# Group normalization on one core: stores and loads issued in runs of two tiles in place of one by one

## The chip, the cores and the metric

One NeuronCore of a Trainium2 chip runs the whole kernel. The metric is the device time in microseconds (us), the median of several executions. The profile is of a single execution, recorded by the hardware profiler; its span (first to last instruction) is 1.7 us shorter than the device time of that execution. With one core there is no second die to compare with. A run counts as slow when it is more than 1.5% above the fastest of its kernel.

## The reference

```python
# x: (128, 1024, 32, 16) bf16, g and b: (1024,) bf16
def reference(x, g, b):
    G = 32
    xr = x.reshape(B, G, C // G, H, W)
    mu = xr.mean(axis=(2, 3, 4), keepdims=True)
    var = ((xr - mu) ** 2).mean(axis=(2, 3, 4), keepdims=True)
    xn = (xr - mu) / jnp.sqrt(var + 1e-5)
    return xn.reshape(B, C, H, W) * g[None, :, None, None] + b[None, :, None, None]
```

Each of the 4096 groups (128 images, 32 groups) has 16,384 values that lie next to each other. Every value is read once and written once: 134.2 MB in, 134.2 MB out.

## The kernel before

The kernel works on 32 tiles. A tile is 4 images by 32 groups, so 128 partitions of 16,384 bf16 values, 4 MB. There are six tile buffers, and a tile is normalized in place: it is loaded into its buffer, worked on there, and stored from it. A buffer can take the next load only when its store has landed.

- PE sums a tile by multiplying it with an identity matrix; DVE reduces the sum to the mean.
- ACT squares the tile in two halves and accumulates.
- POOL and DVE scale 29 of the 32 channels; ACT scales the last three between the two halves of the next tile's squares.
- SP issues every large load and store, in the order of the program. It is one queue in two senses: SP waits in order, and in every trace of this study the large transfers land in the order in which they were issued. Each of them is spread over the core's 16 DMA engines.

The part that sets this order:

```python
XBUFS = 6
UPFRONT = 6
AHEAD = 5
# ...
    for i in range(min(UPFRONT, NT)):      # NT = 32 tiles
        L(i)                               # load a tile
# ...
    def finish(i):                         # called in the middle of ACT's squares of tile i + 1
        if i < 0 or in_parts(i):           # the last two tiles are stored in quarters, elsewhere
            return
        for k in range(KC - LAST_SHARE, KC):
            scale_on("act", i, k)
        S(i, 0, NQ)                        # store the tile
        state.pop(i)
        j = i + AHEAD
        if UPFRONT <= j < NT:
            L(j)
# ...
    for i in range(NT):
        Q(i)                               # squares of tile i; inside it, finish(i - 1)
        if i + 1 < NT:
            M(i + 1)                       # sums of tile i + 1 on PE
            R0(i + 1)                      # its mean on DVE
        V(i)                               # 1/std, scale and shift of tile i
        A(i)                               # scaling on POOL and DVE
```

With S for store and L for load, SP's order is S0, S1, L6, S2, L7, S3, L8 and so on. L7 goes into the buffer of tile 1 and so waits for S1; L6 and S2 stand in the queue between the two. This number of transfers between a store and the load that waits for it is called the cushion below. It is what the DMA engines still have to do when the load is issued. Here it is two.

## Time and profile before

| | |
|---|---|
| device time | 634.2 us |
| span of the profiled execution | 631.9 us |
| share of the span in which the data queue keeps the 16 DMA engines busy | 99.0% |
| busiest computing engine | ACT, 85% |
| rate in mid-span (100 to 550 us) | 432 GB/s |

First some lines of the profile page of the kernel before: busy time by engine; the busy tenths of the DMA engines and what they moved, in 40 slices of the span; the data queue with its share of 16 engines; and the large DMA issues with their median time from issue to landing.

```profile
PE 293.1 (46%) x1025; PEld 114.4 (18%) x1025; DVE 380.2 (60%) x645; ACT 539.0 (85%) x268; POOL 346.8 (55%) x523
...
DMA  8999999999999999999999999999999999999996
GB/s 365 431 437 423 430 431 429 431 433 431 424 430 432 431 431 429 430 433 438 428 432 429 433 431 429 430 430 433 434 431 431 430 430 432 433 426 436 433 418 271
...
q1 hardware_dynamic: 10944, 268.44, 99.0%
...
xt<-in_x_dram SPq DMA_DIRECT2D x30, 4096.0 KB, 29.3
out_dram<-xt SPq DMA_DIRECT2D x30, 4096.0 KB, 38.3
```

No computing engine is full, the DMA engines are. Slices 2 and 3 hold only loads, the middle alternates, the last three hold only stores (the very last also the end, when engines finish), and the rate shows no pattern in this. The same by stretch, from the table of windows of the kernel before (length, then busy time of each engine, the granted clock of PE, the DMA share, GB/s):

```profile
60.00:100.00 40.00, 16.62 (x57) 6.34 (x56) 27.80 (x46) 39.82 (x17) 25.67 (x39) 0.66 1.00 428
100.00:550.00 450.00, 213.12 (x738) 82.58 (x737) 285.44 (x454) 401.73 (x195) 274.86 (x408) 0.72 1.00 432
```

The Trainium skill ("DMA: Bandwidth & Descriptors", Where 436 GB/s comes from) gives the ports a ceiling of 435.2 GB/s; 432 is 99% of that. The "HBM Reference" (Specifications (TRN2)) says that a core that streams alone gets about 425 GB/s, bounded by its 16 DMA engines; the profile's mean over the whole span, start and end included, is 425.

Next, SP's own waits in mid-span (150 to 540 us; total, times, longest) and a piece of SP's timeline (start, duration, instruction), both of the kernel before:

```profile
SPq L101 <- DMA out_dram<-xt: 366.8, 20, 19.0
SPq L381 <- DVE xt L368: 1.5, 1, 1.5
```

```profile
299.30 0.34 SPq L101 DMA_DIRECT2D xt<-in_x_dram  x1
299.75 0.37 SPq L381 DMA_DIRECT2D out_dram<-xt  x1
318.67 0.34 SPq L101 DMA_DIRECT2D xt<-in_x_dram  x1
319.12 0.37 SPq L381 DMA_DIRECT2D out_dram<-xt  x1
```

SP waits nearly always at a load, for a store to land; a store is ready when its turn comes. The store of 299.75 lands after 38.3 us, near 338.1, and the load that waits for it is issued at 338.11. A long wait of SP is no loss by itself here: when it ends, the DMA engines still have two transfers to work on.

PE shows the rhythm in which tiles arrive. Its timeline before (the bracket is its idle time before the piece and what ended that):

```profile
289.61 9.74 PE L166 MATMUL pa<-xt,eye 128*128 128x512 bf16 x32 [10.28 <-DMA xt<-in_x_dram]
309.01 8.58 PE L166 MATMUL pa<-xt,eye 128*128 128x512 bf16 x32 [9.67 <-DMA xt<-in_x_dram]
328.35 9.15 PE L166 MATMUL pa<-xt,eye 128*128 128x512 bf16 x32 [10.75 <-DMA xt<-in_x_dram]
```

One tile comes every 19.4 us, the time of one load and one store.

### The profile page before, as it was taken

How to read it: one execution, taken by the hardware profiler on the slowest of the kernel's cores; microseconds unless marked ns; L12 is line 12 of the kernel's file. 1: busy time of each engine (PE TensorE's matmuls, PEld its weight loads, DVE VectorE, ACT ScalarE, POOL GpSimd, SP SyncE). 2: the span in 40 equal slices, each digit the busy share in tenths (PEclk: the TensorE clock that was granted, in tenths of full speed). 3: DMA queues.
4: the chain of work that ended last, by engine and by line, in shares of the span. 5: the costliest groups of instructions: out<-in, count | busy, mean ns of one | idle time of the engine just before them, and what ended most of it. 6: DMA issues, size and time to landing. Idle time of an engine off the chain costs nothing.

```text
span 631.9 us, 3907 instructions
## 1 busy us (share of the span) xinstructions
PE 293.1 (46%) x1025; PEld 114.4 (18%) x1025; DVE 380.2 (60%) x645; ACT 539.0 (85%) x268; POOL 346.8 (55%) x523
## 2 busy tenths in 40 slices
PE   5578604553245633456433565335553345647000
PEld 2233201221112211122111222112221112213000
DVE  1087666666676576545775457754657654577660
ACT  4589999999999897877997779977989797797960
POOL 0077666666666576544775446764557654477100
PEclk9689758766787657876678766677865788658655
DMA  8999999999999999999999999999999999999996
GB/s 365 431 437 423 430 431 429 431 433 431 424 430 432 431 431 429 430 433 438 428 432 429 433 431 429 430 430 433 434 431 431 430 430 432 433 426 436 433 418 271
DMA packets 11063, 268.70 MB, mean 425 GB/s; under 512 B 1312, under 2 KB 1312, under 8 KB 1312
## 3 DMA queue, kind: packets, MB, share of 16 engines
q1 hardware_dynamic: 10944, 268.44, 99.0%
q8 instruction: 8, 0.13, 0.1%
q14 instruction: 15, 0.12, 0.0%
q10 hardware_dynamic: 96, 0.00, 0.0%
HBM read 134.22 MB, written 134.22 MB: 425 GB/s over the span
## 4 chain that ended last, share of the span: by engine, by line
DMA 67%; ACT 15%; PE 7%; issue 4%; DVE 3%; POOL 0%; SPq 0%; DVEq 0%; ACTq 0%; POOLq 0%
DMA out_dram<-xt 42%; DMA xt<-in_x_dram 25%; ACT ja L244 13%; PE pa L166 7%; DVE xt L368 3%; ACT xt L363 2%; DMA gb_b<-in_g_dram 1%; POOL scl L337 0%; SPq L101 0%; ACT rstd L308 0%; DVE rstd L312 0%; DVE jd L189 0%; POOL shift L343 0%; DVEq L455 0%; DVE bia L324 0%
## 5 line engine op out<-in xcount | busy, mean ns | idle before, releaser
L244 ACT ACTIVATE ja<-xt,negmean 128x8192 fp8e5<-128x8192 bf16 x60 | 426.7, 7112 | 52.1 <-DVE jd L189 52.0
L166 PE MATMUL pa<-xt,eye 128*128 128x512 bf16 x976 | 281.8, 460 | 289.7 <-DMA xt<-in_x_dram 278.5
L368 DVE TENSOR_SCALAR xt<-xt,scl,bia 128x512 bf16<-128x512 bf16 x536 | 352.6, 732 | 40.0 <-POOL bia L353 40.0
L368 POOL TENSOR_SCALAR xt<-xt,scl,bia 128x512 bf16<-128x512 bf16 x390 | 308.7, 806 | 3.4 <-POOL bia L353 0.3
L166 PEld LDWEIGHTS <-eye 128*128 128x128 bf16 x1024 | 114.3, 114 | 468.5 <-DMA xt<-in_x_dram 290.6
L337 POOL TENSOR_SCALAR scl<-gb,rstd 128x32 f32<-128x32 f32 x31 | 11.2, 361 | 218.2 <-DVE rstd L312 218.2
L189 DVE TENSOR_SCALAR_CACHE_REDUCE jd<-pa 128x512 bf16<-128x512 f32 x32 | 22.0, 688 | 149.0 <-PE pa L166 149.0
L363 ACT ACTIVATE xt<-xt,bia,scl 128x512 bf16<-128x512 bf16 x98 | 72.0, 798 | 0.8 <-DVE bia L324 0.8
L244 ACT ACTIVATE ja<-xt,q 128x4096 fp8e5<-128x4096 bf16 x8 | 29.6, 3706 | 6.6 <-DVE jd L189 6.4
L312 DVE RECIPROCAL rstd<-rstd 128x1 f32<-128x1 f32 x32 | 5.1, 160 | 35.8 <-ACT rstd L308 35.8
L343 POOL TENSOR_SCALAR shift<-scl,negmean 128x32 f32<-128x32 f32 x31 | 11.2, 360 | 3.1
L216 POOL TENSOR_SCALAR off<-negmean,q 128x1 f32<-128x1 f32 x2 | 0.9, 432 | 20.5 <-DVE jd L189 20.5
L166 PE MATMUL pb<-xt,eye 128*128 128x512 bf16 x48 | 11.6, 388 | 1.0 <-DMA xt<-in_x_dram 1.0
L308 ACT ACTIVATE rstd<-s,v 128x1 f32<-128x1 f32 x30 | 8.8, 294 | 2.8
L244 ACT ACTIVATION_READ_ACCUMULATOR ja<-xt,negmean 128x1 f32 x60 | 11.2, 187 | 0.0
L353 POOL TENSOR_TENSOR bia<-shift,gb 128x32 f32<-128x32 f32 x31 | 7.8, 252 | 2.6
L308 ACT ACTIVATE rstd<-var,eps_t 128x1 f32<-128x1 f32 x2 | 0.6, 295 | 9.2 <-DVE jv L292 9.2
L273 POOL TENSOR_SCALAR v<-s 128x1 f32<-128x1 f32 x30 | 5.8, 192 | 2.5
L156 DVE COPY gb<-gb_p 128x64 f32<-128x64 f32 x1 | 0.2, 224 | 5.6 <-PE gb_p L148 5.6
L116 ACT ACT_TABLE_LOAD x1 | 1.3, 1283 | 1.7 <-PEq L444 1.7
L189 DVE DVE_READ_ACCUMULATOR jd<-pa 128x1 f32 x32 | 2.6, 81 | 0.0
L292 DVE TENSOR_SCALAR_CACHE_REDUCE jv<-sq,seed 128x4 f32<-128x4 f32 x2 | 0.4, 216 | 2.7 <-ACT ja L244 2.7
(18 smaller groups left out, 6.1 us busy)
## 6 DMA issues: line engine op xcount, KB each, us to landing
xt<-in_x_dram SPq DMA_DIRECT2D x30, 4096.0 KB, 29.3
out_dram<-xt SPq DMA_DIRECT2D x30, 4096.0 KB, 38.3
xt<-in_x_dram SPq DMA_DIRECT2D x8, 1024.0 KB, 16.5
out_dram<-xt SPq DMA_DIRECT2D x8, 1024.0 KB, 17.8
gb_b<-in_g_dram ACTq DMA_DIRECT2D x1, 2.0 KB, 3.2
gb_b<-in_b_dram ACTq DMA_DIRECT2D x1, 2.0 KB, 5.3
```

Source lines behind the costliest of these rows:

```text
L116: chain("act", nc.scalar.activation(out=warm[:], in_=eps_t[:], func=ACT.Sqrt))
L166: nc.tensor.matmul(out=ps[:], lhsT=eye[:], rhs=st["xt"][:, k * MMN : (k + 1) * MMN], start=(k == lo), stop=(k == hi - 1),),
L189: nc.vector.tensor_scalar(out=jd[:], in0=ps[:], scalar1=-inv_n, scalar2=seed, op0=ALU.mult, op1=ALU.add, accum_out=total[:],),
L244: nc.scalar.activation(out=ja[:, 0:w], in_=st["xt"][:, k * w : (k + 1) * w], func=ACT.Square, bias=bias, scale=scale, accum_out=sq, satura ...
L273: nc.gpsimd.tensor_scalar(out=v0[:], in0=s0[:], scalar1=inv_n, scalar2=EPS, op0=ALU.mult, op1=ALU.add,),
L308: nc.scalar.activation(out=rstd[:], in_=last_sum[:], func=ACT.Sqrt, bias=bias[:], scale=scale),
L312: chain("dve", nc.vector.reciprocal(out=rstd[:], in_=rstd[:]))
L337: nc.gpsimd.tensor_scalar(out=scl[:], in0=gam, scalar1=rstd[:], scalar2=None, op0=ALU.mult),
L343: nc.gpsimd.tensor_scalar(out=shift[:], in0=scl[:], scalar1=st["negmean"][:], scalar2=None, op0=ALU.mult,),
L353: nc.gpsimd.tensor_tensor(out=bia[:], in0=shift[:], in1=bet, op=ALU.add),
L363: inst = nc.scalar.activation(out=span, in_=span, func=ACT.Identity, bias=bia, scale=scl)
L368: inst = eng.tensor_scalar(out=span, in0=span, scalar1=scl, scalar2=bia, op0=ALU.mult, op1=ALU.add,)
```

## The change

The intent is to turn the DMA engines' direction half as often: two stores in a row, then two loads in a row.

```diff
 XBUFS = 6
 UPFRONT = 6
-AHEAD = 5
+RUN = 2
@@
         S(i, 0, NQ)
         state.pop(i)
-        j = i + AHEAD
-        if UPFRONT <= j < NT:
-            L(j)
+        if i % RUN == RUN - 1:
+            first = i + 1 + UPFRONT - RUN
+            for j in range(first, min(first + RUN, NT)):
+                L(j)
```

SP's order becomes S0, S1, L6, L7, S2, S3, L8, L9. L6 waits for S0 and L7 for S1, so only one transfer is left between a store and its load.

## The prediction

> **What bounds the kernel now.** The DMA engines. The page gives their data queue 99.0% of the span of 16 engines; by stage (busy time by window) the DMA share is 1.00 from 100 to 550 us at 431 to 433 GB/s, against 85% for ACT, 60% for DVE. The Trainium skill ("DMA: Bandwidth & Descriptors", Where 436 GB/s comes from) puts the port ceiling at 435.2 GB/s; the trace's 431 agrees. 268.44 MB at 431 GB/s are 623 us of the 632 us span; the rest is start, a thinning end (share 0.95 to 0.17 from 622 to 630 us, engines finishing apart) and the last landing.
>
> **Does a change of direction cost anything now?** In the packet records one engine's share of a tile is 8 packets of 1.213 us; landings follow each other every 9.68 us in the alternating stretch, every 9.70 us in the opening loads, which all go one way: no cost per switch to save. By stage, pure loads (12 to 56 us) show 436 GB/s, alternation 431 to 432, pure stores (584 to 622) 417 to 430: no pattern. Slow packets cluster at some switches (the first, near 58 us, about 0.9 us per engine), but all excess over 1.2135 us averages 2.7 us per engine for the run, part of it beside instruction fetches that stay. Halving the switches gives back about 1 us at most.
>
> **What moves.** No work is added or removed; the order on SP becomes S0 S1 L6 L7 S2 S3 L8 L9. Even tiles' loads keep their place, odd ones go one transfer earlier (9.7 us). A load waits on SP for the store 6 tiles back to land (the skill, same page, Anatomy of one DMA: the wait is on the issuing sequencer, the engines just drain their queues; the queue's waits agree: 425 us, 26 times). Now the second load waits for the store just two transfers ahead of it. At its issue only the first load is still queued: 9.7 us of work, where today about two transfers remain (issue to landing: load 29.3, store 38.3 us). The cushion halves, but stays above issue-to-start of about 2 us. Engines run apart by up to 6 us (spread of one transfer's completion records late in the run); the early ones may briefly run dry, the last one, which sets the end, not.
>
> **Compute.** A pair arrives every 38.9 us; ACT needs 16.7 us per tile. By my reckoning a store is ready about 40 us after its own load landed for an even tile, 52 for an odd one (its reciprocal stands on DVE behind the next tile's sum, so behind the next load). The queue reaches them 9 transfers (87 us) after. No store is late. In the tail the last load lands 9.7 us earlier, but tile 30 comes when it did and ACT then takes 16.7 us, so tile 31 is ready near 614 us as now, before the queue needs it.
>
> **Prediction: 634.0 us, 632.3 to 636.5** (8 in 10). Faster by over 2%: 2%; within 2%: 95%; slower: 3%.
>
> **Signs.** Right: queue share 99%, 430 to 433 GB/s in mid-span; second loads' issue to landing near 19 us; PE's waits for loads alternate, one long (20 us), one short; SP still waits mostly for stores to land. Wrong: DMA share under 0.98 in mid-span (cushion too small), SP waiting for DVE in mid-span (stores late), or over 435 GB/s (switches did cost).
>
> **What would make it wrong.** Landings noticed later than I think, so that the queue runs dry once per pair (15 times 1 to 3 us: 650 to 680); a late store; or engines that overlap reading and writing at each switch, so that grouping takes overlap away.

## The result, and the profile after

The changed kernel took 633.6 us (median of four runs, 633.22 to 634.22), the kernel before 634.2 us (634.03 to 634.46). The ratio is 0.999, with a 95% interval of 0.9975 to 1.0004. A ratio here is the mean time of one kernel's fast runs over that of the other's from the same rounds, so it is not quite the ratio of the medians. Five more runs gave the same.

The lines of the page after, in the order of those before:

```profile
PE 260.9 (41%) x1025; PEld 106.4 (17%) x1025; DVE 379.0 (60%) x645; ACT 537.9 (85%) x268; POOL 345.3 (55%) x523
...
DMA  9999999999999999999999999999999999999996
GB/s 371 437 428 406 436 433 431 433 429 433 429 424 433 429 437 431 432 434 433 434 432 424 432 433 431 429 432 432 431 431 431 436 429 432 431 425 435 431 423 260
...
q1 hardware_dynamic: 10944, 268.44, 99.0%
...
xt<-in_x_dram SPq DMA_DIRECT2D x30, 4096.0 KB, 19.4
out_dram<-xt SPq DMA_DIRECT2D x30, 4096.0 KB, 29.3
```

The windows after:

```profile
60.00:100.00 40.00, 16.20 (x55) 6.32 (x55) 26.19 (x45) 39.63 (x20) 24.26 (x39) 0.66 1.01 430
100.00:550.00 450.00, 188.34 (x748) 76.81 (x746) 284.93 (x455) 399.01 (x192) 273.32 (x407) 0.71 1.00 432
```

SP's waits from 150 to 540 us, a piece of its timeline, and PE's timeline, all after:

```profile
SPq L101 <- DMA out_dram<-xt: 367.5, 20, 29.0
SPq L381 <- POOL xt L368: 1.6, 5, 0.5
```

```profile
308.31 9.99 SPq L101 DMA_DIRECT2D xt<-in_x_dram  x2
318.41 0.85 SPq L381 DMA_DIRECT2D out_dram<-xt  x2
348.31 9.94 SPq L101 DMA_DIRECT2D xt<-in_x_dram  x2
358.73 0.82 SPq L381 DMA_DIRECT2D out_dram<-xt  x2
```

```profile
288.93 8.46 PE L166 MATMUL pa<-xt,eye 128*128 128x512 bf16 x32 [21.95 <-DMA xt<-in_x_dram]
298.63 7.08 PE L166 MATMUL pa<-xt,eye 128*128 128x512 bf16 x32 [1.25 <-DMA xt<-in_x_dram]
327.67 9.55 PE L166 MATMUL pa<-xt,eye 128*128 128x512 bf16 x32 [21.96 <-DMA xt<-in_x_dram]
338.57 6.65 PE L166 MATMUL pa<-xt,eye 128*128 128x512 bf16 x30 [1.35 <-DMA xt<-in_x_dram]
```

The form changed as intended: the two loads of a run are issued 10 us apart, each as a store lands, and the two stores follow at once. Tiles come in pairs, so PE waits 22 us, then 1.3 us, where it waited 10 us each time (the window ends within the last of the four pieces, hence its x30). Loads stay in the queue for 19.4 us in place of 29.3, stores for 29.3 in place of 38.3, because less is queued ahead of them. None of this reached the time. The data queue is busy for 99.0% of the span and moves 432 GB/s in mid-span, as before, and SP's total wait for stores is the same to 1 us (367.5 against 366.8).

The 32.2 us less of PE busy time (260.9 against 293.1) is no gain. The second tile of a pair lands 1.3 us after PE has finished the first, and its matmuls run closer together (7.1 us for 32 of them in place of some 9); why they do was not tested. A faster PE does not bring the next tile sooner: PE itself waits for the loads.

### The profile page after: what moved, and what is told of

Read it like the earlier page. It is cut to its first block, busy times and chain, and to the rows that moved or that the text cites. A ratio compares the mean times of both kernels' runs of the same rounds, so it can differ in the third digit from the quotient of the medians.

```text
span 632.5 us, 3907 instructions
## 1 busy us (share of the span) xinstructions
PE 260.9 (41%) x1025; PEld 106.4 (17%) x1025; DVE 379.0 (60%) x645; ACT 537.9 (85%) x268; POOL 345.3 (55%) x523
## 4 chain that ended last, share of the span: by engine, by line
DMA 62%; ACT 15%; PE 9%; issue 5%; DVE 3%; POOL 2%; SPq 0%; DVEq 0%; ACTq 0%; POOLq 0%
DMA out_dram<-xt 40%; DMA xt<-in_x_dram 21%; ACT ja L244 13%; PE pa L166 9%; DVE xt L368 3%; ACT xt L363 2%; POOL xt L368 1%; DMA gb_b<-in_g_dram 0%; ACT rstd L308 0%; POOL scl L337 0%; POOL shift L343 0%; POOL bia L353 0%; SPq L101 0%; DVE rstd L312 0%; DVE jd L189 0%
## 5 line engine op out<-in xcount | busy, mean ns | idle before, releaser
L166 PE MATMUL pa<-xt,eye 128*128 128x512 bf16 x976 | 250.1, 421 | 317.9 <-DMA xt<-in_x_dram 317.9
L166 PEld LDWEIGHTS <-eye 128*128 128x128 bf16 x1024 | 106.3, 106 | 472.2 <-DMA xt<-in_x_dram 318.8
## 6 DMA issues: line engine op xcount, KB each, us to landing
xt<-in_x_dram SPq DMA_DIRECT2D x30, 4096.0 KB, 19.4
out_dram<-xt SPq DMA_DIRECT2D x30, 4096.0 KB, 29.3
```

What stands on the lines that cost most here:

```text
L166: nc.tensor.matmul(out=ps[:], lhsT=eye[:], rhs=st["xt"][:, k * MMN : (k + 1) * MMN], start=(k == lo), stop=(k == hi - 1),),
```

## The experiments

The theory to test: the DMA engines are full, a change of direction costs next to nothing, and the cushion of one transfer is still enough, so the order is free. The rivals: (A) longer runs do save switching time, and the shallower cushion takes it back, so that two effects cancel; (B) longer runs make stores late; (C) computing shares the limit and hides what the order does to the DMA engines.

All twelve results, with the kernel before in the same rounds (634.2 to 634.4 us):

| kernel | time, us | ratio to before, 95% interval |
|---|---|---|
| the change, again | 633.7 | 0.999 (0.9978 to 1.0003) |
| runs of three | 632.8 | 0.998 (0.9968 to 0.9993) |
| runs of four | 654.1 | 1.031 (1.0296 to 1.0331) |
| no cushion | 733.9 | 1.158 (1.1561 to 1.1597) |
| cushion of half a transfer | 681.6 | 1.074 (1.0723 to 1.0756) |
| the same halves, deep queue | 635.8 | 1.002 (1.0004 to 1.0037) |
| no computing: one by one | 633.2 | 0.998 (0.9965 to 0.9992) |
| no computing: two by two | 631.2 | 0.996 (0.9946 to 0.9971) |
| no computing: six by six | 629.0 | 0.991 (0.9899 to 0.9929) |
| no computing: quarters, grouped | 639.4 | 1.008 (1.0066 to 1.0096) |
| no computing: quarters, alternating | 637.8 | 1.005 (1.0039 to 1.0069) |
| no computing, no cushion | 721.3 | 1.137 (1.1358 to 1.1389) |

The kernels without computing copy x to the output; the others gave the right result.

### The change, again

No edit.

> The changed kernel unaltered, for a closer interval beside the other runs: 633 to 634.5 us, ratio 0.997 to 1.001.

It took 633.7 us, ratio 0.999 (0.9978 to 1.0003). Both intervals contain 1.

### Runs of three

```diff
-RUN = 2
+RUN = 3
```

The order S6, S7, S8, L12, L13, L14 has two transfers between a store and its load again, and fewer switches than the change.

> Runs of three: fewer switches still, and again two transfers between a store and the load that waits for it, as in the kernel before. Theory (the DMA engines are full, a switch costs nothing to speak of, stores are never late): 633 to 635 us. Rival A (runs save switching time, and the change's shallower cushion ate the saving): 628 us or less, as the saving comes without the loss. Rival B (longer runs make a store late): over 640, with SP waiting for DVE or ACT in mid-span and a DMA share under 0.99 there.

It took 632.8 us, 1.5 us less than before. Rival A asked for 628 or less and fails; rival B asked for over 640 and fails too, although half of its sign, SP waiting for DVE, did appear. The interval excludes 1, so some 0.2% is real, and this is the fastest of the full kernels. Much of SP's waiting moved from landings to computing (185 us for DVE from 200 to 540 us) without the DMA engines noticing (432 GB/s from 100 to 550 us), as another sign that a wait of SP is not a loss while the queue is deep.

### No computing: one by one, two by two, six by six

The loop over tiles is cut to its transfers; the order on SP stays that of the kernel before, of the change, or of the change with `RUN = 6`. The diff leaves out the calls that prepare the first tile and the definition of `move`.

```diff
     for i in range(NT):
-        Q(i)
-        if i + 1 < NT:
-            M(i + 1)
-            R0(i + 1)
-        V(i)
-        A(i)
+        if in_parts(i):
+            for c in range(NQ):
+                S(i, c, c + 1)
+        else:
+            move(i)          # finish(i) without the scaling
```

> No computing at all (output wrong on purpose: a copy of x), loads and stores in the order of the kernel before. Theory: 628 to 633 us, the full kernel's time less its tail, since the engines' packets are as long as before. Rival C (computing shares the limit, and hides what the order does): 620 us or less. The engines should stay closer together (spread of one transfer's completions under 3 us) if fetches of instructions are what parts them.

> The same without computing, in the order of the change: two stores, two loads. Theory: within 0.3% of the one-by-one order without computing. Rival A or C: the two differ by 1% or more, with two by two faster if switching costs; slower if the cushion of one transfer is too small.

> No computing (output wrong on purpose); six stores, then six loads: some 10 switches in place of about 53. Theory: 629 to 633 us, within 0.5% of the one-by-one and two-by-two orders without computing. Rival A: faster than two by two by 1% or more.

They took 633.2, 631.2 and 629.0 us. Without any computing, one by one is 0.2% faster than the full kernel (at the upper edge of the 628 to 633 us expected, where rival C asked for 620 or less), so rival C fails: computing hides nothing of weight. Two by two and six by six come out 2 and 4 us below one by one. The first is 0.3% and on the edge of what the theory allowed; the second is 0.7% and outside it: a small miss.

The DMA packet records of the traces show where these few microseconds lie. Each engine moves its share of a tile in 8 packets of 1.21 us, in all kernels of whole tiles. What differs is how far apart the 16 engines end:

| kernel | first engine done, us | mean | last | last minus first |
|---|---|---|---|---|
| before | 623.4 | 626.5 | 630.5 | 7.1 |
| the change | 623.8 | 626.7 | 631.2 | 7.4 |
| no computing: one by one | 623.1 | 624.9 | 630.1 | 7.0 |
| no computing: two by two | 623.8 | 625.0 | 628.0 | 4.2 |
| no computing: six by six | 623.6 | 624.2 | 625.8 | 2.1 |

(Times of the packets' ends, from the span's start, found from how many packets run at once near the end: first and last to some 0.1 us, the means to some 0.3 us.) The first engine finishes at the same time in all five. In these five the order does not change the work of an engine that keeps pace; it changes, if anything, how far the slow ones drift behind. Runs of three, which are not in the table, agree: in the landings of each transfer their engines are at most 5.7 us apart, against 7.2 us in the kernel before, a difference of the size that they gain. I had thought that fetches of instructions, which go over the same engines, part them, and expected a spread under 3 us without computing. With 1 fetch packet in place of 23 the one-by-one order still spread to 7.0 us, so that idea fell. Why some engines drift (five of the 16 ended over 2 us behind the others in the one-by-one order) is open.

### Quarters, grouped and alternating

Without computing, all but the opening loads are cut into quarters of 1 MB. One kernel groups four stores, then four loads; the other alternates them. Both load four tiles ahead in place of five, so that the queue is deep for each waiting load: a quarter lands 19.7 us (median) after its issue in both, the time of eight quarters.

```diff
 # grouped -> alternating
         for c in range(NQ):
             S(i, c, c + 1)
+            if load:
+                Lq(j, c)
         state.pop(i)
-        if load:
-            for c in range(NQ):
-                Lq(j, c)
```

> No computing (output wrong on purpose); tiles go in quarters of 1 MB, four quarter stores in a row, then four quarter loads, loads four tiles ahead. A control: as many switches as the kernel before, four times as many transfers. A quarter took 2.45 us against 2.42 for a quarter of a whole tile, so 216 quarters more cost about 6 us: 634 to 642 us.

> The same quarters, but store, load, store, load: 27 x 6 = 162 switches more than the control. Theory (a switch costs next to nothing while the queue is deep): within 0.5% of the control. Rival A (a switch costs time): at the 0.65 us per engine that the first switch after the opening loads cost, it would be 105 us slower; at a tenth of that, 10 us slower.

Grouped took 639.4 us, inside its range, and alternating 637.8 us. The data queue of the two, grouped first:

```profile
q1 hardware_dynamic: 35136, 268.45, 99.8%
q1 hardware_dynamic: 35136, 268.45, 100.0%
```

With 162 more switches the alternating order was not slower but 1.6 us faster. This measures the disputed cost by itself: a switch costs nothing that can be seen while the queue is deep. It also warns against reading a switching cost into the 633, 631, 629 of the last experiment. Rival A fails here most clearly. Only the first turn from loads to stores, near 58 us, stands out in the packet records: packets are longer there by 0.8 us per engine in the kernel before and by 1.2 us after the change. No later stretch of 4 us shows more than 0.3 us, and the cause of the first is open.

### No cushion

```diff
-AHEAD = 5
+AHEAD = 6
```

The order is S6, L12, S7, L13: a load waits for the store issued just before it.

> One store, then one load, but each load now waits for the store issued just before it, so nothing is left in the queue behind that store when the load is issued. If the cushion is what lets the order be free (my theory), each of the 26 waiting loads opens a gap of a landing's notice plus an issue, about 2.4 us by the times between issue and first packet (1.0 us) and between last packet and end (1.4 us) of the kernel before, and the early engines wait for the last as well: 634 + 26 x 2.4 = 696 us, range 665 to 730, with a DMA share near 0.90 in mid-span. If waits of the issuing queue are hidden in some other way, it stays within 2% of 634.

It took 733.9 us, 100 us more than before. The idle gaps came as expected (share 0.91 in mid-span), but the total was above the range, since they are only part of the loss. A piece of SP's timeline, the mid-span window and the data queue of this kernel:

```profile
308.51 0.33 SPq L101 DMA_DIRECT2D xt<-in_x_dram  x1
308.94 0.37 SPq L381 DMA_DIRECT2D out_dram<-xt  x1
332.22 0.33 SPq L101 DMA_DIRECT2D xt<-in_x_dram  x1
332.65 0.37 SPq L381 DMA_DIRECT2D out_dram<-xt  x1
```

```profile
100.00:550.00 450.00, 177.37 (x596) 68.92 (x608) 243.80 (x390) 342.00 (x164) 235.11 (x351) 0.67 0.91 360
...
q1 hardware_dynamic: 10944, 268.44, 91.2%
```

The pattern on SP looks like that of the kernel before, with 23.7 us in place of 19.4 from load to load. Of the 102.5 us by which the profiled span grew (734.4 against 631.9), idle engines make up 58: the data queue was busy for 91.2% of 734.4 us, so idle for 65, against 1.0% of 631.9, which is 6. By the packet records the last completion of a store came at 308.1, and the first packet of the load that waited for it at 309.5. The other 44 us are busy time: 670 us in place of 626, for the same bytes. Around each gap the first packets of the load, and its last ones before the engines turn to the store, took up to 2.6 us in place of 1.21. Over 26 waiting loads that is 2.2 us of idle time, which I had reckoned at 2.4, and 1.7 us of longer packets, which I had not foreseen.

### No computing, no cushion

The same one-line edit in the one-by-one kernel without computing.

> No computing (output wrong on purpose), loads waiting for the store just issued. With computing this order took 734 us: 58 us of it idle engines and 42 us packets longer than 1.21 us. If the longer packets come of the order itself (all engines turning together after a gap), about 730 us again; if they come of the computing engines' traffic, near 690.

It took 721.3 us, nearer to the 730 than to the 690. Its data queue:

```profile
q1 hardware_dynamic: 10944, 268.44, 93.0%
```

That is 93.0% of a span of 719.3 us, so the busy time was 669 us, as with computing. The longer packets thus come of the order itself and not of the computing engines' traffic. Only the idle part is smaller, 50 in place of 65 us; why was not looked into.

### A cushion of half a transfer, and its control

The definition of `Lh`, which loads one half of a tile, is left out of both diffs.

```diff
-        j = i + AHEAD
-        if UPFRONT <= j < NT:
-            L(j)
+        if UPFRONT <= i + 5 < NT:
+            Lh(i + 5, 1)     # second half of a tile's load
+        if i + 6 < NT:
+            Lh(i + 6, 0)     # first half of the next one: waits for S(i)
```

> One store, then the second half of one load and the first half of the next; the first half waits for that store with only half a tile (4.8 us of queue) between. With no cushion a waiting load opened about 2.2 us of idle queue, so 4.8 us should do for the last engine and only hold the early ones back: 632 to 638 us, mid-span DMA share 0.99 or more. If a whole transfer is needed, over 650.

It took 681.6 us, 47 us more than before: a clear miss. Mid-span and data queue of this kernel:

```profile
100.00:550.00 450.00, 201.09 (x680) 75.76 (x679) 261.65 (x416) 367.75 (x177) 252.03 (x374) 0.72 0.99 394
...
q1 hardware_dynamic: 14256, 268.44, 98.0%
```

The DMA share is 0.99, as I had said, and yet the rate is 394 GB/s. The engines were not idle but slow. The queue was busy for 98.0% of 680.7 us, 667 us against 626 before: 41 us of longer packets, and only 7 us more idle time. The first engine's completions show it: the half load that was issued late took mostly 6.3 to 7.4 us in place of 4.86. This is not only the early engines running dry: by the last engine's completions, the late halves took as long (mostly 6.2 to 7.3 us). A share of busy time cannot see this; GB/s can.

The control has the same halves in the same pattern, one tile fewer ahead, so that 2.5 transfers stand between a store and the half load that waits for it:

```diff
-UPFRONT = 6
+UPFRONT = 5
@@
-        if UPFRONT <= i + 5 < NT:
-            Lh(i + 5, 1)
-        if i + 6 < NT:
-            Lh(i + 6, 0)
+        if UPFRONT <= i + 4 < NT:
+            Lh(i + 4, 1)
+        if i + 5 < NT:
+            Lh(i + 5, 0)
```

> The control for the half cushion, which came out at 682 us where I expected 632 to 638: the same halves of loads in the same pattern, but one tile fewer ahead, so that each waiting load has two and a half transfers (24 us of queue) behind the store it waits for. If the shallow queue is what cost 47 us: 633 to 638 us, packets back at their usual length. If the halves or their pattern cost it: near 680 again.

It took 635.8 us. Mid-span of this control:

```profile
100.00:550.00 450.00, 209.27 (x736) 82.46 (x736) 282.69 (x450) 394.90 (x193) 272.54 (x405) 0.73 1.00 430
```

So the halves and their pattern cost 1.4 us, and the shallow queue cost the rest. In this kernel a queue that still holds 4.8 us of work when a load is issued is too shallow; one that holds 9.7 us, as in the change, is deep enough. Nothing between the two was tried.

### Runs of four

```diff
-RUN = 2
+RUN = 4
```

> The full kernel with runs of four: two tiles in hand while four are stored. By my reckoning the last store of each run is ready 1 to 2 us before the queue reaches it, and the last two loads come one store later than now, so tile 31 would be ready some 5 us late: 634 to 645 us. If it is under 634 in spite of that, compute has more slack than I reckon; if over 650, the stores are late in every run, and the DMA share in mid-span falls under 0.98.

It took 654.1 us, above my range. SP's waits from 150 to 540 us in this kernel:

```profile
SPq L381 <- DVE xt L368: 320.6, 20, 29.4
SPq L101 <- DMA out_dram<-xt: 55.3, 10, 9.4
```

and three windows of it, the opening, mid-span and the tail:

```profile
60.00:100.00 40.00, 9.04 (x34) 3.48 (x32) 27.22 (x45) 39.82 (x18) 25.07 (x38) 0.65 0.83 357
100.00:550.00 450.00, 190.03 (x754) 77.73 (x755) 267.68 (x428) 374.50 (x182) 258.09 (x385) 0.72 1.00 423
610.00:640.00 30.00, 0.17 (x1) 0.00 (x0) 21.70 (x60) 28.58 (x21) 7.72 (x14) 0.58 0.76 321
```

SP now waits for DVE, that is, for tiles to be ready for their store: in the order of four, the loads stand behind a store that is not computed yet. In mid-span the last store of a run is issued when the queue is nearly empty: one at 254.36 us, while the store before it landed between 254.7 us (first engine) and 258.0 us (last). The opening loses 7 us (share 0.83 over 40 us: the seventh load waits for tile 3 to be computed), the tail another 7 (0.76 over 30 us), and mid-span is 2% slower at a full share, 423 against 432 GB/s, which is 9 us of 450. This is where rival B comes true: between three and four tiles in a run, with six buffers. I had looked for the loss in mid-span's share of busy time, and that sign missed it; as with the half cushion, GB/s shows it.

## Why the prediction was right

- **The bound.** Right. The data queue's share was 99.0% and the mid-span rate 432 GB/s before and after, and the kernel without any computing is only 1 us faster (633.2 against 634.2, ratio 0.998).
- **A switch costs nothing to speak of; halving them gives back about 1 us at most.** Right. The change gave 0.5 us, not clear of noise, and 162 more switches in the quarters cost nothing (637.8 against 639.4 us).
- **The cushion halves, and stays large enough.** The conclusion was right: the share stayed at 1.00, and the loads landed 19.3 to 20.6 us after their issue (200 to 540 us). The reason given was too weak. I compared 9.7 us of queued work with an issue-to-start of about 2 us (the gap shown above, without a cushion, had its first packets 1.0 to 2.1 us after the issue), which would make 4.8 us safe as well. The experiment says no: 4.8 us cost 47 us, mostly as longer packets in a queue that was hardly ever empty. The margin of the change was smaller than I thought, and that 9.7 us lay on the safe side of it was in part luck.
- **Early engines may run dry briefly, the last one not.** Not seen to matter. The spread at the end, 7.4 us, is that of the kernel before, 7.1 us.
- **No store is late.** Right. In mid-span SP waited 1.6 us in total for computing. The trace bears out the reckoning itself: from tile 14 to tile 29, even tiles were scaled 39 to 40 us after their load landed, odd ones 51 to 52 us, where 40 and 52 were predicted. My reckoning for longer runs was too kind: I put runs of four at 634 to 645 us and they took 654.
- **The tail.** Right. The last store was issued at 615.0 us (554.94 + 60.10 in SP's timeline) against 614.65 before.
- **Signs.** PE's waits alternate between 22 and 1.3 us, where 20 and a short one were predicted.
- **What would have made it wrong.** A queue that runs dry in each pair would have given 650 to 680 us by my text. Kernels with a shallow queue at every tile in fact reached 682 (half a transfer) and 734 us (none).

What stays open: why packets get longer when a load is issued into a nearly empty queue, and why some DMA engines drift up to 7 us behind the others in the one-by-one order without computing and only 2 us in the six-by-six order.

## What to carry to other kernels

If the DMA engines are at 99% and move the same GB/s in stretches of loads alone, stores alone and both, expect little from reordering transfers: here at most 0.7% (six by six without computing) and 0.2% in a full kernel. Read that rate by stage before you try. The order was free only while the queue stayed deep: count the transfers between a store and the load that waits for its buffer. Here one whole 4 MB transfer (9.7 us of work) was enough and half of one was not. Judge a change of order by GB/s as well as by the DMA engines' busy share, since a shallow queue slowed this kernel by 7% with the share at 0.99.

## What the Trainium skill lacked or had wrong

- "DMA: Bandwidth & Descriptors" (Where 436 GB/s comes from) says that for transfers between HBM and SBUF the HBM side, about 358 GB/s, binds. With one core active the runs moved 432 GB/s in mid-span in both directions mixed; the port ceiling of 435.2 is what fits. Only that sentence is off for a core that runs alone: the same section calls a measurement of 425 GB/s near the rate of the ports. The "HBM Reference" (Specifications (TRN2)), which says that a core alone gets about 425, agrees with the whole-span mean of 425.
- No page says how deep the queue must be. "DMA: Bandwidth & Descriptors" (Anatomy of one DMA) gives a fixed cost of about 2.0 us for DMAs issued by GpSimd and says that waits happen on the issuing sequencer while the engines just consume their queues. The idle time per load without a cushion, 2.2 us, is close to it, though these loads were issued by SP. But 4.8 us of queued work was not enough (682 us), 9.7 us was (634 us), and most of that loss (41 of 48 us) was packets that took longer, not idle engines.
- No page says whether a change between reading and writing costs an engine time. In a deep queue it does not: 637.8 us with the switches, 639.4 us with 162 fewer.
- "DMA: Bandwidth & Descriptors" (Latency and other measured facts) says that DMA engines 7 and 15 are usually slower, and ties its best guess, which it calls uncertain, to the descriptor rings of another issue path (GpSimd's). Here all large transfers were issued from SP, and the last engine still ended up to 7.4 us after the first. The packet records do not tell which engines these were.
